# Top-k attention and a low-rank mixer on one core: weighted values of two tiles formed in one go, transposes of u moved two shares

## The chip, the cores and the metric

The kernel runs on one core of a Trainium2 chip. The metric is the device time of one execution in microseconds (us); a kernel's time is the median over its runs. Engines are named as in the profile: PE is TensorE (matmuls; PEld are its weight loads, which overlap them), DVE is VectorE, ACT is ScalarE, POOL is GpSimd, SP is SyncE, which here only issues DMAs. Each engine works through its own queue in the order in which the program gave it work, and waits on semaphores for the others.

## The reference

Attention in which each query keeps only its 32 largest scores, then a mixer over the sequence of rank 32 and a two-layer network over the channels. Eight batches, eight heads, 576 positions, 64 channels a head.

```python
def _attn_ref(q, k, v):                       # (8, 8, 576, 64) each
    scores = scale * np.matmul(q, k.transpose(0, 1, 3, 2))
    kth = np.partition(scores, -32, axis=-1)[..., -32:-31]
    scores = np.where(scores >= kth, scores, -1000000000.0)
    attn = np.exp(scores - np.max(scores, axis=-1, keepdims=True))
    attn = attn / (np.sum(attn, axis=-1, keepdims=True) + 1e-09)
    return np.matmul(attn, v)

def _moe_ref(x, U, V, w_ch1, w_ch2):          # x: heads side by side, (8, 576, 512)
    h = x.transpose(0, 2, 1) @ U @ V          # U (576, 32), V (32, 576)
    u = x + h.transpose(0, 2, 1)
    ch = np.maximum(u @ w_ch1, 0.0) @ w_ch2   # 512 -> 2048 -> 512
    return u + ch
```

## The kernel before

**Tiles and steps.** Heads are taken in pairs g = 0 to 31, four pairs to a batch. The 576 queries of a pair are cut into tiles t = 0 to 3 of 128 rows, for both heads, and a tile 4, the tail, that holds the last 64 rows of both heads. The list `steps` gives each step n one tile; from pair 4 on, tiles 3 and 4 share a step, so that a pair has four steps (`ALONE` = 20 is the first of these). The loop over n at the end of the kernel is an order written out by hand: it emits, in program order, work of several tiles, each at another stage.

**A tile's way.** In step n the loop forms the scores of tile n+1 (`scores`: PE, L336, and L368 for the tail; ACT copies them out, L381, L401, L404), folds each row in two halves (`fold` and `split`: POOL L432, DVE L434, POOL L435), finds the 32 largest of the rows of tile n on DVE (`front`: maxima L487, L502, L520, and replacements L485, L515), and masks and weighs tile n-1 (ACT L546 and L549, POOL L550, ACT L439). DVE turns the weights of tile n-1 in blocks (`blocks`, L576), SP writes them to DRAM (L582), and in the next step ACT's queue fetches them back as PT (`back`, L591). PT has two buffers. In step n PE also forms the weighted values of tile n-3.

**Weighted values.** `weighted(m)` is called early in step m+3, after the first `fill`, with `values` for each tile of step m. `values` takes an accumulator O from the PSUM pool `ps_t` (two buffers, shared by all transposes and by the low-rank products), adds one product over the last 64 keys of both heads with vd (L688, all 128 rows and columns of the array), then eight with va, each for one head and so for 64 columns of the array (L691), and ACT copies O into XT (L700). For the tail there are ten products of 64 columns (L662, ACT L669). Each fp32 product counts as two matmul records in the profile.

**The mixer of a pair.** After the tail's values `weighted` appends `mixed(g, None, 1)` to the list `mixing`. It is a generator that each `fill` moves on by one `yield`: one share of delay (`lag`), then POOL multiplies XT with the inverse sums of the weights into uT (L719 twice, L720 for the tail), then two shares of delay, then PE transposes uT (L725 four times, L738 for the tail) and ACT copies it to X (L729, L739). It then waits until the next `weighted` is done, whereupon PE forms the product with U (pT, L750), and in the next two shares those with V (up, L762), which ACT copies (L777) and POOL adds to uT (L778). With the last pair of a batch uT is whole, and the layers of this batch, `mlp(b)`, go into the list `fillers`.

**Shares of the layers.** Each step calls `fill` eight times. A call adds a share to `due` and then emits matmuls of the layers (first layer L810, second L828, each with a relu or a copy on ACT, L823 and L839; L840 on POOL adds u) until `due` is used up. Twelve layer matmuls after a column block is done, its transposes back are emitted (L852, ACT L854 and L856, SP L858), also through `ps_t`. A share is 1.0227 products of 512 columns; it is multiplied by 1.4 (`LONG`) in the step of tiles 3 and 4, and by 0.91 (`EARLY`) up to step 38. The layers of the last batch are done differently (`closing`), after the last step.

Of the kernel before, what the change touches and what calls it, by code (L numbers as in the profile page):

```python
# [26 lines left out]
def kernel(  # L27
# [35 lines left out]
    NT, TAIL = 4, 64  # L63
# [7 lines left out]
    ALONE = NPAIR * CH  # L71
# [59 lines left out]
    def cols(t):  # L131
        return slice(t * P, t * P + rows(t))
# [4 lines left out]
    def half(h):  # L137
        return slice(h * D, (h + 1) * D)
# [511 lines left out]
                sc[half(h), MAIN:S], rd[2 * NT : 2 * NT + 1, half(h)].to_broadcast([D, TAIL])  # L650
            )

    def values(g, t):

        PT = PTs.pop((g, t))
        va, vd, vt = (a[g % NV] for a in (vas, vds, vts))
        O = ps_t.tile([P, P], F32, tag="tp", name="O")
        if t == NT:
            if g >= NPAIR:
                for j in range(NT + 1):  # L660
                    for h in range(2):
                        nc.tensor.matmul(  # L662
                            O[half(h), 0:TAIL],
                            lhsT=va[:, h, j, :] if j < NT else vt[:, h, :],
                            rhs=PT[:, j, half(h)],
                            start=(j == 0),
                            stop=(j == NT),
                        )
                nc.scalar.copy(XTs[g][:, MAIN:S], O[:, 0:TAIL])  # L669
                return  # L670
            den = dens[g]
            if g not in inverted:
                inverse(g, 2 * NT if g == NPAIR - 1 else 0, 2 * NT + 1)
            for j in range(NT + 1):
                nc.tensor.matmul(
                    O,
                    lhsT=PT[:, j],
                    rhs=va[:, :, j, :] if j < NT else vt,
                    start=(j == 0),
                    stop=(j == NT),  # L680
                )
            for h in range(2):
                nc.scalar.mul(X[half(h), NT, half(h)], O[half(h), half(h)], den[half(h), 2 * NT :])
            return
        if shared(g, t):
            PT = PT.rearrange("p c n -> p (c n)")
            PT = PT.rearrange("p (a c j) -> p c a j", a=4, j=BLK)
        nc.tensor.matmul(O, lhsT=vd, rhs=PT[:, 2 * NT], start=True, stop=False)  # L688
        for j in range(NT):
            for h in range(2):  # L690
                nc.tensor.matmul(  # L691
                    O[half(h)],
                    lhsT=va[:, h, j, :],
                    rhs=PT[:, NT * h + j],
                    start=False,
                    stop=(j == NT - 1),
                )
        if t == 0:
            XTs[g] = attn.tile([P, S], F32, tag="XT", name="XT", bufs=1)
        nc.scalar.copy(XTs[g][:, cols(t)], O)  # L700


    def mixed(g, wait, lag=0):

        for _ in range(lag):
            yield
        b, gi = divmod(g, NPAIR)
        if gi == 0:
            uTs[b] = mlpp.tile([P, NC, S], F32, tag="uT", name="uT")
        XT, den = XTs.pop(g), dens[g]  # L710
        uT = uTs[b][:, gi]
        if g >= NPAIR:
            sc = scales.pop(g)
            pairs_ = [
                a[:, 0:MAIN].rearrange("p (b n) -> p b n", b=2) for a in (XT, sc)
            ]
            ends = [uT[:, OFF[t] : OFF[t] + 2 * P] for t in (0, 2)]
            for i, end in enumerate(ends):
                nc.gpsimd.tensor_tensor(end, pairs_[0][:, i], pairs_[1][:, i], ALU.mult)  # L719
            nc.gpsimd.tensor_tensor(uT[:, at(NT)], XT[:, MAIN:S], sc[:, MAIN:S], ALU.mult)  # L720
            yield
            yield
        tp = ps_t.tile([P, NT, P], F32, tag="tp", name="tp")
        for t in range(NT):
            nc.tensor.transpose(  # L725
                tp[:, t, :], XT[:, cols(t)] if g < NPAIR else uT[:, at(t)], ident
            )
        X4 = X[:, 0:NT, :]
        nc.scalar.copy(X4, tp)  # L729
        if g < NPAIR:  # L730
            X4 = X4.rearrange("p t (h d) -> p t h d", h=2)
            den4 = den[:, 0 : 2 * NT].rearrange("p (t h) -> p t h ()", h=2)
            nc.gpsimd.tensor_tensor(X4, X4, den4.to_broadcast([P, NT, 2, D]), ALU.mult)
        else:
            if g == NPAIR:
                nc.gpsimd.memset(X[TAIL:P, NT, :], 0.0)
            tp = ps_t.tile([P, P], F32, tag="tp", name="tp")
            nc.tensor.transpose(tp[0:TAIL], uT[:, at(NT)], ident)  # L738
            nc.scalar.copy(X[0:TAIL, NT, :], tp[0:TAIL])  # L739
        if wait is None:  # L740
            waiting.append(g)
            while g in waiting:
                yield
        else:
            for _ in range(wait):
                yield
        pT = ps_t.tile([P, P], F32, tag="tp", name="pT")
        for t in range(NT + 1):
            i = t % NT * R
            nc.tensor.matmul(  # L750
                pT[i : i + R, :],
                lhsT=U[:, t, :],
                rhs=X[:, t, :],
                start=(t < NT),
                stop=(0 < t),
            )
        Tb = mlpp.tile([P, P], F32, tag="Tb", name="Tb", bufs=1)
        nc.scalar.copy(Tb, pT)
        yield
        for chunks, (lo, hi) in zip(PARTS, SPAN):  # L760
            up = ps_t.tile([P, WIDE], F32, tag="tp", name="up")
            nc.tensor.matmul(  # L762
                up[:, 0 : hi - lo], lhsT=Tb, rhs=V[:, lo:hi], start=True, stop=(g >= NPAIR)
            )
            for t in chunks if g < NPAIR else ():
                nc.tensor.matmul(
                    up[:, OFF[t] - lo : OFF[t] - lo + rows(t)],
                    lhsT=X[:, t, :],
                    rhs=ident if t < NT else ident2,
                    is_transpose=True if t < NT else None,  # L770
                    start=False,
                    stop=(t == chunks[-1]),
                )
            if g < NPAIR:
                nc.scalar.copy(uT[:, lo:hi], up[:, 0 : hi - lo])
            else:
                nc.scalar.copy(sc[:, lo:hi], up[:, 0 : hi - lo])  # L777
                nc.gpsimd.tensor_tensor(uT[:, lo:hi], uT[:, lo:hi], sc[:, lo:hi], ALU.add)  # L778
            yield
        if gi == NPAIR - 1:  # L780
            fillers.append(closing(b) if b == B - 1 else mlp(b))
# [340 lines left out]
    steps = [[(g, t)] for g in range(NPAIR) for t in range(CH)]  # L1122
    for g in range(NPAIR, NP):
        steps += [[(g, t)] for t in range(NT - 1)] + [[(g, NT - 1), (g, NT)]]
    STEPS = len(steps)
    BATCH = NPAIR * NT


    SLOTS, LONG, EARLY = 8, 1.4, 0.91
    share = MLP_WORK / (NPAIR * SLOTS * (NT - 1 + LONG))  # L1130
    fillers, mixing, due = [], [], 0.0

    def fill(k=1):


        nonlocal due
        for _ in range(k):
            if passes:
                passes.pop(0)()
            if mixing and next(mixing[0], True):  # L1140
                mixing.pop(0)
            due += share * (LONG if len(tiles(n)) > 1 else 1) * (EARLY if n <= ALONE + BATCH + 2 else 1)
            while due > 0:
                if not fillers:
                    due = 0.0
                    break
                done = next(fillers[0], None)
                if done is None:
                    fillers.pop(0)
                else:  # L1150
                    due -= done

    def tiles(n):

        return steps[n] if 0 <= n < STEPS else []

    def weighted(m):

        for g, t in tiles(m):
            values(g, t)  # L1160
        if tiles(m)[-1][1] == NT:
            mixing.append(mixed(g, None, 1) if m < STEPS - 1 else mixed(g, 5, 0))

# [12 lines left out]
    t = 0  # L1176
# [5 lines left out]
    for n in range(STEPS + 2):  # L1182
        if n < STEPS:
            g, t = steps[n][0]
# [9 lines left out]
        if n >= ALONE - 1 and n <= ALONE:  # L1194

            if n < ALONE:
                next(last)
                values(*steps[n - 3][0])
                list(turning)
                next(here)  # L1200
                next(last)
                scores(*steps[n + 1][0])
                fold(*steps[n + 1][0])
                values(*steps[n - 2][0])
            list(turns(*steps[n - 1][0]))
            values(*steps[n - 1][0])
            if n < ALONE:
                split(*steps[n + 1][0])
                next(here)
# [25 lines left out]
        if n < ALONE:  # L1235
# [3 lines left out]
            scores(*steps[n + 1][0])  # L1239
            fold(*steps[n + 1][0])  # L1240
            if n >= 3:
                values(*steps[n - 3][0])
                if (n - 3) % CH == NT:
                    mixing.append(mixed((n - 3) // CH, 3))
            list(turning)
# [111 lines left out]
```

## Time and profile before

| | us |
|---|---|
| median of three runs | 1681.74 (1681.38 to 1683.37) |
| the profiled execution | 1681.84 |
| its span, first to last instruction | 1679.8 |
| busy: PE, DVE, POOL, ACT | 1571.6, 1547.1, 1000.2, 991.1 |
| layers: L810, L828 | 461.7, 462.1 |
| values: L691 | 144.6 |
| scores: L336 | 179.0 |

A row of the profile's groups gives busy time, the mean of one instruction, and the idle time of its engine just before such instructions with what ended it. Matmuls are pipelined, and their modelled ends overlap the next starts: what a run of them costs is read from start to start. A waits row reads: who waited, for whom, microseconds in total, times, longest. The idle time of one engine costs time only where that engine sets the pace.

### The profile page before, as it was taken

What the parts mean: (1) busy time and instruction counts of PE and PEld (TensorE: products, weight loads), DVE (VectorE), ACT (ScalarE), POOL (GpSimd) and SP (SyncE); (2) the same over time, 40 slices, a digit from 0 to 9 for tenths busy, and PEclk for the clock granted to TensorE, in tenths of its full rate; (3) what the DMA queues carried; (4) which work ended last, traced back from release to release, by engine and by line L of the source; (5) the groups of instructions that cost most, each with busy time, mean ns of one, the idle gap of its engine ahead of it and who ended that gap; (6) DMA issues with size and microseconds to landing.
All of it is one profiled execution on the core that took longest, in us unless ns stands there. A gap on an engine that the chain in (4) does not pass through costs nothing.

```text
span 1679.8 us, 30303 instructions
## 1 busy us (share of the span) xinstructions
PE 1571.6 (94%) x9638; PEld 1183.9 (70%) x9638; DVE 1547.1 (92%) x4393; ACT 991.1 (59%) x2475; POOL 1000.2 (60%) x853
## 2 busy tenths in 40 slices
PE   4667698999899999999999999999999999999999
PEld 2444466687667786778777887778777887778776
DVE  7999998999999999999999999999999999994452
ACT  4888788665665556565655656565655656564320
POOL 4778668755666565666566565656666565653620
PEclk7787799999999999999999999999999999999999
DMA  3323232255555555555455455555555555543001
GB/s 87 94 76 97 62 94 73 63 135 132 134 128 135 127 142 132 139 127 138 121 134 137 124 146 132 137 128 136 126 130 136 126 149 132 131 120 110 10 1 28
DMA packets 295631, 189.42 MB, mean 113 GB/s; under 512 B 178768, under 2 KB 279984, under 8 KB 295472
## 3 DMA queue, kind: packets, MB, share of 16 engines
q1 hardware_dynamic: 259728, 117.62, 30.2%
q10 hardware_dynamic: 35744, 69.88, 13.7%
q8 instruction: 76, 1.25, 0.3%
q14 instruction: 83, 0.68, 0.1%
HBM read 116.49 MB, written 70.91 MB: 112 GB/s over the span
## 4 chain that ended last, share of the span: by engine, by line
PE 58%; DVE 25%; POOL 5%; DMA 4%; ACT 3%; issue 2%; SPq 2%; ACTq 0%; DVEq 0%; POOLq 0%
PE mm L828 17%; PE mm L810 16%; DVE m L520 7%; DVE upper L515 7%; PE sc L336 5%; PE O L691 5%; PE mm L904 3%; DVE first L502 2%; DVE y L576 2%; DVE upper L487 2%; PE sc L904 2%; PE tp L904 2%; DMA ld<-in_k_dram 2%; POOL uT L719 2%; PE up L762 1%
## 5 line engine op out<-in xcount | busy, mean ns | idle before, releaser
L550 POOL TENSOR_TENSOR Ssb<-Ssb,E 128x576 f32<-128x576 f32 x243 | 339.9, 1419 | 248.3 <-ACT E L549 247.8
L810 PE MATMUL mm<-uT,w 128*128 128x320 f32 (+1 forms) x1792 | 461.7, 410 | 2.4 <-ACT hT L823 2.0
L828 PE MATMUL mm<-hT,w 128*128 128x320 f32 (+1 forms) x1792 | 462.1, 407 | 0.0
L810 PEld LDWEIGHTS mm<-uT,w 128*128 128x128 f32 x1792 | 335.4, 191 | 103.0 <-issue 11.6
L828 PEld LDWEIGHTS mm<-hT,w 128*128 128x128 f32 x1792 | 332.3, 190 | 93.0 <-issue 10.2
L520 DVE MAX8 m<-upper 128x8 f32<-128x304 f32 (+1 forms) x780 | 367.3, 512 | 0.7
L515 DVE MATCH_REPLACE8 upper<-m,upper 128x304 f32<-128x304 f32 (+1 forms) x520 | 259.9, 507 | 0.0
L432 POOL TENSOR_TENSOR lower<-Ssb 128x576 uint32<-128x576 uint32 x108 | 152.6, 1413 | 139.1 <-ACT Ssb L381 52.2
L439 ACT ACTIVATE Ssb<-Ssb,nmax 128x576 f32<-128x576 f32 x258 | 201.4, 783 | 17.6 <-POOL Ssb L526 9.9
L435 POOL TENSOR_TENSOR lower<-lower,upper 128x576 uint32<-128x576 uint32 x108 | 153.1, 1418 | 74.2 <-DVE upper L434 72.6
L336 PE MATMUL sc<-qkT 64*128 64x288 f32 (+1 forms) x1056 | 179.0, 461 | 11.0 <-ACT Ssb L390 7.8
L487 DVE MAX8 upper<-lower 128x8 f32<-128x288 f32 x432 | 172.3, 440 | 10.7 <-POOL lower L435 10.7
L549 ACT ACTIVATE E<-Ssb,least 128x576 f32<-128x576 f32 x243 | 176.2, 769 | 4.2
L381 ACT COPY Ssb<-sc 128x576 f32<-128x576 f32 x216 | 127.6, 643 | 71.4 <-PE sc L336 71.4
L576 DVE STREAM_TRANSPOSE y<-Ssb 128x512 f32<-128x512 f32 (+1 forms) x312 | 153.9, 545 | 0.0
L823 ACT ACTIVATE hT<-mm 128x320 f32<-128x320 f32 (+1 forms) x224 | 91.9, 411 | 102.1 <-PE mm L810 100.9
L691 PE MATMUL O<-PT,va 128*64 128x128 f32 x2048 | 144.6, 285 | 0.0
L336 PEld LDWEIGHTS sc<-qkT 64*128 64x128 f32 (+1 forms) x1056 | 95.9, 197 | 51.7 <-issue 17.1
L691 PEld LDWEIGHTS O<-PT,va 128*64 128x64 f32 x2048 | 113.4, 141 | 16.4 <-issue 2.0
L700 ACT COPY XT<-O 128x128 f32<-128x128 f32 x128 | 33.8, 264 | 111.3 <-PE O L691 103.8
L515 DVE MATCH_REPLACE8 upper<-first,upper 128x304 f32<-128x304 f32 x216 | 97.7, 460 | 0.0
L485 DVE MATCH_REPLACE8 lower<-upper,lower 128x288 f32<-128x288 f32 x216 | 94.1, 444 | 0.0
(264 smaller groups left out, 2258.3 us busy)
## 6 DMA issues: line engine op xcount, KB each, us to landing
away<-y SPq DMA_DIRECT2D x416, 144.0 KB
PT<-away ACTq DMA_DIRECT2D x104, 576.0 KB
raw<-in_moe_w_ch_dram SPq DMA_DIRECT2D x32, 512.0 KB
va<-in_v_dram SPq DMA_DIRECT2D x64, 128.0 KB
out_dram<-ob SPq DMA_DIRECT2D x59, 128.0 KB
scale<-rd ACTq DMA_DIRECT2D x56, 128.0 KB
ld<-in_q_dram SPq DMA_DIRECT2D x108, 64.0 KB
ld<-in_k_dram SPq DMA_DIRECT2D x108, 64.0 KB
```

The lines of the kernel that those rows point to most:

```text
L336: nc.tensor.matmul(out, lhsT=qkT[half(h), 0, cols(t)], rhs=qkT[half(h), 1, lo:hi], start=True, stop=True,)
L435: nc.gpsimd.tensor_tensor(bottom, bottom, top.bitcast(U32), ALU.subtract)
L439: nc.scalar.activation(E, chunk, AF.Exp, bias=nmax, scale=SCALE, accum_out=total)
L487: nc.vector.max(spot, lower)
L515: nc.vector.match_replace(nxt, ms[c], curs[c], NEG)
L520: nc.vector.max(ms[c], curs[c])
L549: nc.scalar.activation(gap, chunk, AF.Relu, bias=least[:, c : c + 1], scale=-WIDEN)
L550: nc.gpsimd.tensor_tensor(chunk, chunk, gap, ALU.subtract)
L576: nc.vector.transpose(y[:, :, i * NT : i * NT + c].rearrange("p r c j -> p c r j"), E2[:, a : a + c * P].rearrange("p (c r j) -> p c r j", ...
L691: nc.tensor.matmul(O[half(h)], lhsT=va[:, h, j, :], rhs=PT[:, NT * h + j], start=False, stop=(j == NT - 1),)
L810: nc.tensor.matmul(ph[:, 0:w], lhsT=first_layer(cc, f), rhs=uT[:, cc, lo:hi], start=(cc == 0), stop=(cc == NC - 1),)
L828: nc.tensor.matmul(po[:, 0:w], lhsT=w2[:, f, c * P : (c + 1) * P], rhs=hTs[f][:, 0:w], start=(f == 0), stop=(f == NF - 1),)
```

## The change

Three things change in the steps from pair 4 on.

*Values of two tiles.* `values` takes several tiles; its body is now a generator, `valued`, that stops once after the product with vd. For all tiles but a tail the products with vd come first, one after the other, each into its own O; then each tile's products with va follow, and its copy. `weighted` now only keeps the tile in `held` when it is tile 0 or 2 of its pair, and at the next step forms the values of both (tiles 0 and 1, or 2, 3 and 4). The last two steps are formed as before.

*Transposes of u.* In `mixed` the delay between POOL's products and PE's transposes is four shares in place of two, for all but the last pair.

*Shares.* `weight(n)` replaces the factor of a share: from step 24 to the last, 0.18 is taken off it in steps of tile 0 and 2 of a pair, and put on in those of tile 1 and 3. Values that were formed in a step of tile 1 or 3 are those now formed a step later, in one of tile 2 or 0.

```diff
-    def values(g, t):
+    def valued(g, t):
...
+        yield
         for j in range(NT):
             for h in range(2):
                 nc.tensor.matmul(
...
         nc.scalar.copy(XTs[g][:, cols(t)], O)
-
+        yield
+
+
+    def values(*tiles_):
+
+        jobs = [valued(*tile_) for tile_ in tiles_]
+        for job, (_, t) in zip(jobs, tiles_):
+            if t < NT:
+                next(job)
+        for job in jobs:
+            next(job)
...
-            yield
-            yield
+            for _ in range(4 if wait is None else 2):
+                yield
...
+    HEAVY = 0.18
+
+    def weight(n):
+
+        long = LONG if len(tiles(n)) > 1 else 1
+        if n < ALONE + NT or n >= STEPS:
+            return long
+        return long + (-HEAVY if steps[n][0][1] in (0, 2) else HEAVY)
...
-            due += share * (LONG if len(tiles(n)) > 1 else 1) * (EARLY if n <= ALONE + BATCH + 2 else 1)
+            due += share * weight(n) * (EARLY if n <= ALONE + BATCH + 2 else 1)
...
+    held = []
+
     def weighted(m):
 
-        for g, t in tiles(m):
-            values(g, t)
+        g, t = tiles(m)[0]
+        held.extend(tiles(m))
+        if t in (0, 2) and m < STEPS - 2:
+            return
+        values(*held)
+        held.clear()
         if tiles(m)[-1][1] == NT:
             mixing.append(mixed(g, None, 1) if m < STEPS - 1 else mixed(g, 5, 0))
```

The other calls of `values` (pairs 0 to 3, one tile at a time) are only rewritten for its new form.

## The prediction

> **What bounds the kernel now.** I read the page first: busy shares, then the forty slices.
>
> ```profile
> span 1679.8 us, 30303 instructions
> ...
> PE 1571.6 (94%) x9638; PEld 1183.9 (70%) x9638; DVE 1547.1 (92%) x4393; ACT 991.1 (59%) x2475; POOL 1000.2 (60%) x853
> ...
> PE   4667698999899999999999999999999999999999
> ...
> DVE  7999998999999999999999999999999999994452
> ```
>
> Two engines are full together from the eighth slice (about 300 us) to the 36th (1512 us). Only in the last slices does DVE run empty while PE goes on. Shares over a whole run hide which of the two waits, so next come the busy times of two stretches of 189.2 us, the period in which the trace repeats itself: one batch, that is four pairs of heads (columns: stretch, length, then busy time of PE, PEld, DVE, ACT, POOL, granted clock, DMA share, GB/s).
>
> ```profile
> 756.20:945.40 189.20, 187.59 (x1189) 143.13 (x1188) 186.14 (x565) 112.24 (x284) 113.85 (x97) 1.00 0.53 133
> 945.40:1134.60 189.20, 187.60 (x1189) 143.13 (x1188) 186.10 (x565) 112.24 (x284) 113.88 (x97) 1.00 0.53 133
> ```
>
> Of 189.2 us DVE idles 3.1, PE by this view 1.6. The change takes no work from DVE: a batch can't become shorter than 186.1 us. Third, who waits, from 300 to 1536 us: the DVE's waits, and the PE's.
>
> ```profile
> DVE upper L434 <- ACT Stail L401: 12.1, 10, 1.9
> DVE upper L487 <- POOL lower L435: 6.2, 7, 1.9
> ```
>
> ```profile
> PE tp L725 <- POOL uT L719: 11.9, 35, 3.1
> PE mm L810 <- ACT hT L823: 2.0, 3, 1.3
> PE O L688 <- DMA PT<-away: 1.0, 1, 1.0
> ```
>
> DVE waits 18.3 us in all, two thirds of it at L434 for scores that PE had just formed. So PE sets the pace, DVE close behind. PE's own waits are nearly all at one line, the transposes of u, L725. Idle time understates them, as a matmul's modelled end runs on; the starts say more. The timeline of PE around one such place (start, length, engine, line):
>
> ```profile
> 704.17 1.24 PE L336 MATMUL sc<-qkT 64*128 64x288 f32 x8
> 705.34 2.96 PE L828 MATMUL mm<-hT,w 128*128 128x320 f32 x10
> 708.46 0.44 PE L725 MATMUL tp<-ident,uT 128*128 128x128 f32 x2 [0.16 <-POOL uT L719]
> 709.16 0.44 PE L725 MATMUL tp<-ident,uT 128*128 128x128 f32 x2 [0.26 <-POOL uT L719]
> 709.44 0.30 PE L738 MATMUL tp<-ident,uT 128*64 128x128 f32 x1
> 709.58 3.40 PE L828 MATMUL mm<-hT,w 128*128 128x320 f32 x12
> 712.81 0.49 PE L852 MATMUL tp<-ident,oT 128*128 128x128 f32 x3
> 713.14 1.78 PE L828 MATMUL mm<-hT,w 128*128 128x320 f32 x6
> 714.75 0.38 PE L688 MATMUL O<-PT,vd 128*128 128x128 f32 x2
> 715.07 1.09 PE L691 MATMUL O<-PT,va 128*64 128x128 f32 x16
> ```
>
> Twelve L828 last 3.23 us from start to start (709.58 to 712.81), so one is 0.27 and the ten before L725 need 2.70: L725 could start at 708.04 and starts at 708.46, 0.42 late. Three transposes of L852 take 0.33 (712.81 to 713.14), so four need 0.44; here L725 to L738 is 0.98, another 0.54. **Loss: 0.96 us a pair.** What is late is POOL, in the all-engine timeline of the same place:
>
> ```profile
> 704.97 1.18 ACT L381 COPY Ssb<-sc 128x576 f32<-128x576 f32 x2 [1.65 <-PE sc L336]
> ...
> 706.28 1.42 POOL L432 TENSOR_TENSOR lower<-Ssb 128x576 uint32<-128x576 uint32 x1 [1.35 <-DMA away<-y]
> ...
> 707.65 1.46 POOL L719 TENSOR_TENSOR uT<-XT,scale 128x256 f32<-128x256 f32 x2
> ...
> 709.03 0.35 POOL L720 TENSOR_TENSOR uT<-XT,scale 128x64 f32<-128x64 f32 x1
> ```
>
> PE's scores (until 705.41) release ACT's copy L381 (until 706.15), that releases POOL's L432, and behind it in POOL's queue stand L719 twice and L720 (until 709.38). The transposes need all three. The loop starts and ends on PE, so it isn't DVE's doing.
>
> **The change, part by part.** *Transposes two shares later.* Today three shares (fill 2 to 4) lie between the scores and L725; after it five, but each is 0.82 of itself, since this is a step of tile 2. A whole share is 1.0227 columns-of-512, 2 x 0.432 us each (a 320-wide matmul pair lasts 0.54, so 512 columns 0.86): 0.88 us. Three whole shares are 2.65, five of 0.82 are 3.62: L725 comes 0.96 us later after the scores, and L720, the last thing it needs, is 0.96 late today. It just covers. Matmuls come whole (0.54 or 0.43), so some pairs keep a few tenths; bounds of the saving 0.5 and 0.96, I take 0.85 (the arithmetic lies near the upper end). What is moved with them: ACT's copies L729 and L739 (0.59 and 0.26), and the three shares after. The next reader, pT (L750), is at 716.09 today, 5.7 us after L739 ends. After the change two light shares, one of 1.58 and no values stand between: 2 x 0.72 + 1.39 = 2.8 us, against 1.1 for the two copies. No DMA and no POOL work moves.
>
> *Values of two tiles together.* No matmul is added or removed. From start to start: L688 (two, full array) 0.32 to L691, where two full-array matmuls of 128 columns alone would be 0.22 (L852: 0.109 each): 0.10 goes at the change of array shape. L691 to L336 or L750 is 1.02 (715.07 to 716.09), but to L662, which has the same shape, 0.92 to 0.93 (701.38 to 702.31): again 0.10. Two tiles apart: 2 x (0.32 + 1.02) = 2.68; together 0.22 + 0.32 + 0.92 + 1.02 = 2.48. Against that the light step now goes from full-array layers straight into scores of 64 rows, a passage that the trace doesn't hold. Bounds of the net saving per two tiles: 0 (it costs two such changes) to 0.20 (nothing); I take 0.10, one change more, as both passages seen cost that. That is 0.2 us a pair. The Trainium skill, TensorEngine Tiling (Array Packing), section Key Properties, says that changing the tiling mode, not just the tile, drains the array; by it the light step pays too and 0.10 is right, while the two rows alone would promise 0.20. *Buffers:* O takes both buffers of ps_t at once, and the tail a third; ACT's copy L700 (0.26) must free the first before L662. Today's rows: values start at 701.07, so the first tile's end would be 702.5, the second's 703.45; L700 runs from 702.64 to 702.89. Cover 0.5 us; if ACT is later, PE waits, and behind it the tail scores, then L434. The Trainium skill, TensorEngine Tiling (Array Packing), section PSUM Bottleneck, warns that tiling speeds up TensorE but not the emptying of PSUM, which speaks against holding two accumulators; by it the cover would be gone and a pair 0.26 us worse, where the row (0.26 us in a gap of 0.92) says nothing is lost. PT's row for tile 0 is held a step longer, and ACT's DMA into that buffer (L591) then waits for values that stand ahead of L381's scores in PE's order, so L381, ahead of it on ACT, covers it. XT's one buffer is refilled for tile 0 a step later than today, behind L720 all the same. SP's loads of va and vd go into the buffers of three pairs back, whose values are done either way.
>
> *Shares dealt.* Per pair the weights still sum to 4.4. A step is 7.07 us of layers by weight 1; 0.18 is 1.27 us, about the 1.24 to 1.34 of a tile's values. So scores in steps 0 and 2 keep their place, and those in 1 and 3 come 2 to 3 us earlier (values gone, and the lighter shares before them). PE waits there if DVE's L434 hasn't freed the scores' buffers: L434 ends at 707.43, the next scores are at 716.65, elsewhere at least 5.2 us after. Enough.
>
> **Sum.** PE per pair -0.85 - 0.2 = -1.05, per batch 189.2 - 4.2 = 185.0, below DVE's 186.1. So DVE takes over and the gain is what DVE waits today. L434's 12.1 us I count in full: PE gains 1.05 a pair, and the largest wait, about 1.6, comes once in four pairs. L487's 6.2 I count by half: POOL's L435 stands behind L840, which hangs on ACT's DMA issues as well as on PE. Gain 12.1 + 3.1 = 15.2: span 1664.6. The profiled execution took 1681.84, 2.0 above its span (median of the runs 1681.74): **1666.6, say 1667 us.** What follows the last step is PE's closing with the same work, and moves up whole. Its own range: from all 18.3 us won and 2 more at the end, where DVE stands 6.5 us at L629 (1661) to half of L434's (1675).
>
> **Rivals.** *Transposes still wait* (the change doesn't do what it says): smaller shares eat the delay, 0.2 to 0.35 us a pair remain as gain. For it: the cover is exact to 0.0. Against: every wait shortens by what L725 is moved. 27 pairs x 0.2 to 0.35 = 5 to 9, so about 1675. *DVE holds its waits* (gain hidden anyway): DVE is at 98.4%, and waits at L487 hang on POOL. For it: from 331 to 565 us DVE waits nowhere. Against: L434's waits follow PE's scores directly. 2 to 3 us off, 1680. *The third accumulator* (slower): at the step of tile 2 the tail's O waits for L700, which on ACT stands behind L546 and two L549 (1.65 us), and these for DVE's last maxima. For it: the less PE waits elsewhere, the further it runs ahead of DVE, and so of ACT. Against: cover 0.5 us, and a lead of PE that is lost there costs DVE nothing at first. It decides from 0.5 + 1.05 us of lateness on; at 2 us, 27 x (2 - 0.5 - 1.05) = 12: 1694.
>
> **Chances.** Forecast 0.66, transposes still wait 0.14, DVE holds its waits 0.08, third accumulator 0.12. A measurement of this kernel tells 0.2% (3.4 us) from no change: faster 0.80, same 0.08, slower 0.12. The range 1661 to 1680 leaves out the slower case, half of the unchanged one and a little at the bottom.
>
> **What would show it.** Right: no wait at L725, DVE over 99.5% busy in a batch of some 186.5 us, L434's waits gone, PE waiting here and there for ACT or for scores' buffers. L688 four in a row at every other step, L691 to L691 0.92. Wrong: new waits of L662 or L688 on L700, L750 on L739, or a batch still near 189 us with DVE's waits moved to the scores after three tiles' values.

## The result, and the profile after

The changed kernel takes 1697.19 us in the median (1691.11 to 1702.04), the kernel before 1681.5 in the same measurement: a ratio of 1.0093, 95% interval 1.0082 to 1.0104. It is slower where 1667 us was forecast, and its runs spread over 11 us where those of before spread over 3. The profiled execution took 1691.11, its span 1689.0. It is the fastest of the six, so the profile can show 9.2 of the 15.7 us that the medians lie apart.

The page of the changed kernel, busy shares and slices:

```profile
span 1689.0 us, 30294 instructions
...
PE 1558.2 (92%) x9638; PEld 1179.3 (70%) x9638; DVE 1548.1 (92%) x4393; ACT 986.0 (58%) x2475; POOL 1001.6 (59%) x853
...
DVE  7999997999999999999999999999999999994452
```

PE's busy time is 13.4 us shorter than before, and yet the end comes 9.2 us later. A batch of four pairs (columns: stretch, length, busy time of PE, PEld, DVE, ACT, POOL, granted clock, DMA share, GB/s):

```profile
763.00:952.40 189.40, 185.56 (x1190) 142.45 (x1188) 186.01 (x564) 111.11 (x285) 114.11 (x96) 1.00 0.54 133
```

It takes 189.4 us, of which DVE works the same 186.0. From one L434 to the one four pairs on, batches take 187.4 to 191.0 us, before 187.5 to 189.5. So in the middle of the run nothing was won. Where the 9 us were lost shows in the start of L434 for tile 3 of single pairs, in both traces:

| before, us | after, us | later by |
|---|---|---|
| 331.3 | 336.4 | 5.1 |
| 377.8 | 385.7 | 7.9 |
| 754.8 | 764.5 | 9.7 |
| 1133.1 | 1141.9 | 8.7 |
| 1511.5 | 1520.2 | 8.7 |

Nearly all of it is lost by 380 us; from there on L434 of tile 3 is 7.4 to 10.6 us later than before. The DVE's waits, and the PE's, from 300 to 1545 us:

```profile
DVE upper L434 <- ACT Stail L401: 22.5, 15, 4.0
DVE upright L629 <- ACT den L560: 1.6, 1, 1.6
DVE upper L487 <- POOL lower L435: 0.4, 1, 0.4
```

```profile
PE mm L823 <- ACT hT L836: 22.9, 16, 2.3
PE tp L738 <- POOL uT L732: 2.6, 1, 2.6
```

The line numbers have moved: L823 is the first layer (L810 before), L836 its relu (L823 before), L738 the transposes of u (L725 before). Those wait no more, but 22.9 us of waits for a relu stand in their place, and DVE's waits for the tail's scores have grown from 12.1 to 22.5 us. One belongs to the other. The chain of waits around one such place, in order of time (start, length, what):

```profile
749.72 0.59 SPq L258
750.32 0.04 issue
750.36 5.07 DMA ld<-in_k_dram
755.42 0.02 issue
755.45 0.49 ACTq L649
755.93 0.05 issue
755.98 0.20 ACT nmax L506
756.19 0.28 ACT hT L836
756.47 0.04 issue
756.51 1.56 PE mm L823 x6
758.07 0.45 PE O L690 x4
758.52 1.90 PE O L694 x32
760.42 0.58 PE O L662 x20
761.00 1.18 PE sc L368 x14
762.18 0.71 PE sc L336 x4
762.89 0.02 issue
762.91 1.18 ACT Ssb L381 x2
764.09 0.39 ACT Stail L401
764.48 0.02 issue
764.50 0.76 DVE upper L434
```

It starts at a load of k. ACT's queue in the same stretch:

```profile
752.80 0.62 ACTq L645 DMA_DIRECT2D scale<-rd  x1
755.45 0.49 ACTq L649 DMA_DIRECT2D scale<-rd  x1
755.98 0.20 ACT L506 ACTIVATE nmax<-first 128x2 f32<-128x2 f32 x1 [3.50 <-DMA ld<-in_k_dram]
756.09 0.64 ACT L836 ACTIVATE hT<-mm 128x256 f32<-128x256 f32 x2
```

In the step of tile 1, now a light one (it forms no values; its shares of the layers are the larger ones, of 1.18), ACT issues four DMAs that fetch the inverse sums (`scale`, L645 and L649 twice). Three follow each other at 0.66 us. The fourth stands for 2.0 us, until 755.45. It needs nothing of k: the program tells the end of its DMAs by eight semaphores in turn, and this DMA gets the one that the load of k issued at 750.36 used last. That load's last update is at 755.42, 0.02 us before ACT goes on. Behind it in ACT's queue stand two relus. PE has two buffers for its layers, both full, and stands 1.75 us. The time that PE was to win in the light step is lost, and the heavy step comes: values of three tiles, then the tail's scores, then L434, which has waited 1.80 us when it starts at 764.50.

In the changed kernel the fourth DMA stands in 23 of 26 pairs, 43.5 us in all; before it stood in 9 of 27, 13.9 us. Each of these stands ends 0.02 us after the DMA that used its semaphore last has landed: in the changed kernel 17 times a load of k, and 6 times ACT's own fetch of PT (L591); before, 3 and 6 times. Twelve of PE's 16 waits for a relu, some 20 of the 22.9 us, end 1.0 to 1.3 us after such a DMA goes out. Before, the semaphore had mostly been used last by a load of k that had landed already. The four DMAs of one such pair before:

```profile
790.65 0.62 ACTq L645 DMA_DIRECT2D scale<-rd  x1
791.31 0.63 ACTq L649 DMA_DIRECT2D scale<-rd  x1
791.97 0.62 ACTq L645 DMA_DIRECT2D scale<-rd  x1
792.63 0.62 ACTq L649 DMA_DIRECT2D scale<-rd  x1
```

The load in question was issued at 788.36, 2.3 us ahead of the first of the four, and had landed at 790.80. In the changed kernel the lead is 1.1 us (750.36 to 751.49): ACT's DMAs follow the load sooner, and the fourth meets it still under way.

### The profile page after: what moved, and what is told of

Read it like the earlier page. It is cut to its first block, busy times and chain, and to the rows that moved or that the text cites. A ratio compares the mean times of both kernels' runs of the same rounds, so it can differ in the third digit from the quotient of the medians.

```text
span 1689.0 us, 30294 instructions
## 1 busy us (share of the span) xinstructions
PE 1558.2 (92%) x9638; PEld 1179.3 (70%) x9638; DVE 1548.1 (92%) x4393; ACT 986.0 (58%) x2475; POOL 1001.6 (59%) x853
## 4 chain that ended last, share of the span: by engine, by line
DVE 60%; PE 18%; DMA 10%; SPq 5%; ACT 2%; issue 2%; POOL 1%; ACTq 1%; DVEq 0%; POOLq 0%
DVE m L520 15%; DVE upper L515 14%; DVE y L576 7%; DMA ld<-in_k_dram 6%; DVE upper L487 6%; DVE first L502 5%; DVE lower L485 4%; DVE place L515 3%; PE mm L917 3%; PE mm L841 3%; DVE upper L434 3%; PE mm L823 3%; DVE qkT L306 2%; PE O L694 2%; PE tp L917 2%
## 5 line engine op out<-in xcount | busy, mean ns | idle before, releaser
L823 PE MATMUL mm<-uT,w 128*128 128x320 f32 (+1 forms) x1792 | 464.2, 410 | 23.0 <-ACT hT L836 22.9
L823 PEld LDWEIGHTS mm<-uT,w 128*128 128x128 f32 x1792 | 334.4, 191 | 127.0 <-ACT hT L836 32.2
L520 DVE MAX8 m<-upper 128x8 f32<-128x304 f32 (+1 forms) x780 | 376.9, 537 | 0.7
L515 DVE MATCH_REPLACE8 upper<-m,upper 128x304 f32<-128x304 f32 (+1 forms) x520 | 266.1, 532 | 0.0
L435 POOL TENSOR_TENSOR lower<-lower,upper 128x576 uint32<-128x576 uint32 x108 | 153.0, 1417 | 187.8 <-DVE upper L434 187.7
L439 ACT ACTIVATE Ssb<-Ssb,nmax 128x576 f32<-128x576 f32 x258 | 201.5, 783 | 32.1 <-POOL lower L432 13.9
L487 DVE MAX8 upper<-lower 128x8 f32<-128x288 f32 x432 | 176.1, 459 | 4.3 <-POOL lower L435 4.3
L549 ACT ACTIVATE E<-Ssb,least 128x576 f32<-128x576 f32 x243 | 176.4, 769 | 4.3
L836 ACT ACTIVATE hT<-mm 128x320 f32<-128x320 f32 (+1 forms) x224 | 90.3, 409 | 89.1 <-PE mm L823 81.4
L694 PE MATMUL O<-PT,va 128*64 128x128 f32 x2048 | 132.4, 282 | 0.0
L434 DVE TENSOR_TENSOR upper<-sc,Ssb 128x576 f32<-128x576 f32 x108 | 83.0, 769 | 24.4 <-ACT Stail L401 24.4
```

The lines of the kernel that those rows point to most:

```text
L439: nc.scalar.activation(E, chunk, AF.Exp, bias=nmax, scale=SCALE, accum_out=total)
L487: nc.vector.max(spot, lower)
L515: nc.vector.match_replace(nxt, ms[c], curs[c], NEG)
L520: nc.vector.max(ms[c], curs[c])
L549: nc.scalar.activation(gap, chunk, AF.Relu, bias=least[:, c : c + 1], scale=-WIDEN)
L694: nc.tensor.matmul(O[half(h)], lhsT=va[:, h, j, :], rhs=PT[:, NT * h + j], start=False, stop=(j == NT - 1),)
```

## The experiments

Theory A: the loss comes from ACT, held by that DMA in the light step, so that PE can't lay up time for the heavy one. Theory B: values of three tiles ahead of the tail's scores make L434 late whatever ACT does. Medians and ratios are each against the kernel before on the same chip.

**Transposes alone**, an edit of the kernel before.

```diff
-            yield
-            yield
+            for _ in range(4 if wait is None else 2):
+                yield
```

> The kernel before with four shares of delay in place of two ahead of the transposes of u (L725), nothing else changed. Theory A (the loss comes from ACT: in the light step of tile 1 it now stands at the fourth of its DMAs for the inverse sums until a load of k has landed, relus behind it, so PE cannot use the light step) and theory B (the loss comes from the order: values of three tiles ahead of the tail's scores make L434 late whatever ACT does) agree here: PE's waits at L725 go, 0.85 to 0.96 us a pair, DVE takes over, 1667 to 1673 us. If the moved transposes are themselves the cause of the loss, 1690 us or more.

Measured: 1686.38 us, ratio 1.0025 (1.0012 to 1.0037). Neither faster nor the cause of the whole loss. Its waits, DVE's and PE's, from 300 to 1545 us:

```profile
DVE upper L434 <- ACT Stail L401: 12.2, 7, 4.5
DVE upper L487 <- POOL lower L435: 7.5, 6, 2.6
```

```profile
PE mm L810 <- ACT hT L823: 14.1, 11, 3.3
PE O L688 <- DMA PT<-away: 6.4, 7, 1.6
```

The waits at L725 are gone here too (3.3 us left, 3.1 of it at one place), and DVE waits as long as before. Instead ACT's fourth DMA now stands in 19 of 27 pairs, 32.8 us, and PE waits for relus. The expectation of both theories was wrong: this wait holds PE without any pairs of tiles and without dealt shares.

**Pairs of tiles and dealt shares alone** (the two `yield`s of before put back into the changed kernel).

> The changed kernel with the two shares of delay of before: values of two tiles together and shares of 0.82 and 1.18 alone. A and B: slower than before, and slower than the changed kernel by up to the L725 waits, 1695 to 1715 us, L434 waiting at the step of tile 2. If the pairs cost nothing by themselves, within 5 us of 1681.

Measured: 1707.15, ratio 1.0154 (1.0137 to 1.0171). As expected: with PE waiting for the transposes again (25.0 us), L434 waits 38.2.

**Even shares**, from here on edits of the changed kernel where nothing else is said.

```diff
-    HEAVY = 0.18
+    HEAVY = 0.0
```

> The changed kernel with HEAVY 0: all shares as before, so heavy steps are 1.3 us longer on PE and light ones 1.3 us shorter. B: the scores after the values of three tiles come 1.3 us later still, once or twice a pair for 27 pairs, 1715 to 1740 us. A: PE reaches the light step's DMAs later by nothing and finds them blocked as often, PE's waits at L823 as in the changed kernel, 1695 to 1715. If the dealt shares are the cause of the loss, 1665 to 1680.

Measured: 1705.79, ratio 1.0147 (1.0117 to 1.0177). The dealt shares are worth some 8 us to the changed kernel, less than B asked for and within A's range; they aren't its fault.

**The four DMAs at the end of the step.**

```diff
-        if n < STEPS and n - 2 >= ALONE and len(tiles(n - 2)) > 1:
-            scale(steps[n - 2][0][0])
         next(here, None)
         next_params(1)
...
         next(here, None)
         fill()
+        if n < STEPS and n - 2 >= ALONE and len(tiles(n - 2)) > 1:
+            scale(steps[n - 2][0][0])
         fill()
```

> The changed kernel with the four DMAs for the inverse sums (L645, L649) issued by ACT at the end of the step, ahead of its last share, in place of ahead of L506. A: the waits of two to three us at the fourth of them go, with them PE's waits at L823 (22.9 us) and most of L434's (22.5 us): 1668 to 1682 us. B: PE's waits at L823 may go, L434 still waits: 1688 to 1702.

Measured: 1685.12, ratio 1.0023 (1.0014 to 1.0032): 12 us of the 16 return. That lies between the ranges of A and B. PE's waits for relus fall from 22.9 to 2.8 us, for A, but L434 still waits 14.9 us for the tail's scores (22.5 in the changed kernel). Another wait of PE takes the relus' place:

```profile
PE O L662 <- ACT XT L703: 14.5, 15, 2.1
PE O L690 <- DMA PT<-away: 3.2, 3, 1.3
```

L662 is the tail's values, L703 ACT's copy of the accumulator of tile 2 (L700 before): the third accumulator waits for a buffer of `ps_t`, as the issues of four DMAs now stand just ahead of L546 and L549 on ACT.

**Only the fourth DMA at the end of the step.** The first three stay; `ends_` is the L649 of before.

```diff
+    fourths = []
...
-            nc.scalar.dma_start(
+            ends_ = lambda h=h: nc.scalar.dma_start(
                 sc[half(h), MAIN:S], rd[2 * NT : 2 * NT + 1, half(h)].to_broadcast([D, TAIL])
             )
+            if h == 0 or g == NP - 1:
+                ends_()
+            else:
+                fourths.append(ends_)
...
         fill()
+        while fourths:
+            fourths.pop()()
         fill()
```

> The changed kernel with only the fourth of the four DMAs (the second L649) moved to the end of the step; the first three stay. If the wait of this one DMA for the load of k is what costs (theory A), it gives what moving all four gave, 1683 to 1688 us. If the issue time of four DMAs on ACT (0.66 us each) at that place is what costs, only a quarter of it, 1692 to 1699.

Measured: 1673.62, ratio 0.9960 (0.9946 to 0.9975). **One DMA of 16 KB, moved by three shares, is worth some 22 us** by the ratios; the changed kernel is then faster than before. That is 9 us under the range of theory A, which had taken over the time of the run above, and far from the 1692 us and more that four issue times would leave. The DMA still stands (22 of 27 pairs, 35.3 us), but L506 and the relus of three shares stand ahead of it in ACT's queue, no longer behind. With three issues fewer ahead of L546 and L549 PE waits 4.4 us for the third accumulator in place of 14.5, and L434 5.6 us for the tail's scores. The waits of PE in this kernel (L829 is the first layer, L668 the tail's values):

```profile
PE mm L829 <- ACT hT L842: 4.7, 7, 1.8
PE O L668 <- ACT XT L709: 4.4, 7, 1.0
```

**The DMAs' place in the kernel before**: the move of the four, in the kernel before.

> The kernel before with the four DMAs for the inverse sums issued at the end of the step, nothing else changed. There the fourth stands two to three us in one pair of four, without a PE wait behind it. Theory A: worth 0 to 4 us, 1678 to 1682. If the DMAs' place is worth as much to the kernel before as to the changed one (12 us), 1670.

Measured: 1678.08, ratio 0.9979 (0.9968 to 0.9990), as expected. The place by itself is worth 3 us there; PE still stands at L725 (14.3 us, 43 times).

**Transposes and late DMAs**, no pairs.

> The kernel before with four shares of delay ahead of the transposes of u and the four DMAs at the end of the step. Theory A: in the run with the transposes alone PE's waits only moved from L725 (43.9 us with its weight loads) to the relus behind these DMAs (L810, 14.1 us); with both gone DVE takes over and its waits fall under 8 us: 1668 to 1675. If the forecast of DVE taking over was wrong for another reason, 1680 to 1687.

Measured: 1664.69, ratio 0.9890 (0.9866 to 0.9915), 13.4 us below the run just above and 3 us under theory A's range. Two batches of it, and DVE's waits at L434 and L487 from 300 to 1545 us:

```profile
749.10:935.30 186.20, 185.37 (x1187) 143.32 (x1187) 185.94 (x566) 111.65 (x284) 113.28 (x97) 1.00 0.52 135
935.30:1121.10 185.80, 185.80 (x1191) 143.92 (x1190) 185.66 (x565) 112.38 (x287) 114.06 (x97) 1.00 0.53 136
```

```profile
DVE upper L434 <- ACT Stail L401: 2.7, 2, 2.1
DVE upper L487 <- POOL lower L435: 0.4, 1, 0.4
```

A batch takes 186.0 us and DVE is busy for 185.8 of them: now it sets the pace, as forecast.

**Transposes and only the fourth DMA late.**

> The kernel before with four shares of delay ahead of the transposes of u and only the fourth DMA at the end of the step. Theory A: as with all four moved, 1663 to 1668 us. If ACT's issue time counts: 1670 to 1680.

Measured: 1663.84, ratio 0.9900 (0.9884 to 0.9917). As with all four, so it is the one DMA's wait and what is queued behind it. This kernel and the one above are among the fastest; their intervals overlap.

**Pairs of tiles from pair 6 on** (pairs 4 and 5 turn their weights on PE, through `ps_t`).

```diff
-        if t in (0, 2) and m < STEPS - 2:
+        if t in (0, 2) and ALONE + 2 * NT <= m < STEPS - 2:
...
-        if n < ALONE + NT or n >= STEPS:
+        if n < ALONE + 3 * NT or n >= STEPS:
```

> The changed kernel, but tiles are formed together and shares dealt only from pair 6 on (pairs 4 and 5 as before; these turn their weights on PE through the two buffers of ps_t). The trace of the changed kernel has lost 5.1 us against before by 331 us and 7.9 by 378 us. If that comes from two accumulators against the turns of pairs 4 and 5, some 4 to 6 us return: median 1690 to 1693 us. If it comes from the order of values and scores in any pair, nothing returns: 1695 to 1699.

Measured: 1687.61 (1681.43 to 1694.35), ratio 1.0032 (1.0011 to 1.0052). That is 10 us below the changed kernel's first measurement and 2 us under the lower of the two ranges; the spread of both kernels is as large, so the size is uncertain.

**Late DMAs and pairs from pair 6 on.**

> The changed kernel with the DMAs at the end of the step and pairs of tiles from pair 6 on, the tail's accumulator as in the change (a third buffer). Moving the DMAs alone gave 1685.1 us, all three mends 1665.2. The late DMAs alone had lost 8.0 us by 331 us: if that is pairs 4 and 5, 1675 to 1679, and the rest (10 us) is the third accumulator.

Measured: 1674.61, ratio 0.9969 (0.9956 to 0.9982); 9 to 10 us below the late DMAs alone (by the ratios, by the medians). PE still waits 10.8 us for the third accumulator.

**Late DMAs and two buffers for three accumulators.** The tail's accumulator is the second half of tile 3's, and ACT copies tile 3 after the tail's products.

```diff
+    rests = {}
...
-        O = ps_t.tile([P, P], F32, tag="tp", name="O")
+        if t == NT and g >= NPAIR:
+            O = rests.pop(g)
+        else:
+            both = ps_t.tile([P, 2, P], F32, tag="tp", name="O")
+            O = both[:, 0]
+            if t == NT - 1 and g >= NPAIR:
+                rests[g] = both[:, 1]
...
+        if t == NT - 1 and g in rests:
+            yield
...
+        for job in jobs:
+            next(job, None)
```

> The changed kernel with the DMAs at the end of the step and the tail's accumulator in the second half of tile 3's, pairs of tiles from pair 4 on as in the change. If the third accumulator is worth 10 us beside the late DMAs: 1673 to 1678, with PE's 14.5 us at L662 gone. If pairs 4 and 5 are all that is left: 1684.

Measured: 1668.99, ratio 0.9933 (0.9918 to 0.9948). 15 to 16 us from the accumulator beside the late DMAs, where 10 were expected, and the wait for it is gone. L434 waits 2.4 us for the tail's scores, with pairs of tiles from pair 4 on.

**All three mends.**

> The changed kernel with three mends: the DMAs at the end of the step, pairs from pair 6 on, and the tail's accumulator in the second half of tile 3's, so that two buffers hold all three (ACT copies tile 3 after the tail's products). In the run with the late DMAs alone PE waited 14.5 us for a third buffer and lost 8 us by 331 us. If these are what is left of the loss: 1668 to 1676. If L434's waits come from the three tiles' values themselves: 1680 to 1686.

Measured: 1665.24, ratio 0.9898 (0.9869 to 0.9928), 3 us under the first range. DVE's waits for the tail's scores, from 300 to 1540 us:

```profile
DVE upper L434 <- ACT Stail L401: 2.7, 2, 2.2
```

They are down to 2.7 us with the values of three tiles still ahead of those scores. Theory B falls: that order is harmless where PE can lay up time. And the mended pairs bring nothing beyond the transposes (1664.69): by then DVE sets the pace.

## Why the prediction was wrong

**Right, by the runs.** The loss at L725 and its mending: the waits went from 11.9 to 2.6 us. No run shows a batch under 185.8 us, and with the four DMAs late the transposes gave 13.4 us (1678.08 to 1664.69), near the 15.2 of the sum. Also the terms on array shape. PE of the changed kernel at a light step:

```profile
744.09 1.89 PE L823 MATMUL mm<-uT,w 128*128 128x256 f32 x8
745.92 1.24 PE L336 MATMUL sc<-qkT 64*128 64x288 f32 x8
```

Eight matmuls of 0.216 are 1.73 us, the scores start after 1.83: the passage straight into scores of 64 rows costs 0.10, as taken.

**The step that failed** is the end of *Shares dealt*: that in light steps PE could only be held by the scores' buffers, "Enough". The forecast looked for what holds PE itself, and not for what holds ACT, on which PE's layers hang by two buffers. The change brought ACT sooner after the load to a DMA issue whose wait is set by another transfer, and there ACT stood, and PE behind it. The dealt shares aren't needed for it: with the transposes alone the fourth DMA stands 32.8 us in place of 13.9, so "No DMA and no POOL work moves" in *Transposes two shares later* failed in the same way. No DMA changed its place in a queue, but their times against each other did. In the sum it is the sentence "So DVE takes over and the gain is what DVE waits today": of the 1.05 us a pair that PE was to save (28 us in 27 pairs) 22.9 stand again as waits for relus. The sum named ACT's DMA issues, at L487, as a thing that POOL's L840 hangs on, ahead of L435, counted half of 6.2 us for it, and didn't ask what their wait was; in the before trace it could be seen in 9 pairs of 27.

**The rivals.** That of the third accumulator was real, but small in the changed kernel: 0.4 us at L662 from 300 us on, and one wait ahead of that, at the first tail formed this way:

```profile
280.93 0.69 PE L662 MATMUL O<-PTt,va 128*64 128x64 f32 x16 [1.94 <-ACT XT L703]
```

It came out when the four DMAs were moved (14.5 us, and 15 to 16 us of time when this was mended too). Most of that came from their new place ahead of L546 and L549: with only the fourth moved it is 4.4 us. So the rival had the right place and the right order on ACT, but needed these issues for its size. "Transposes still wait" was wrong: L725's waits went, and no time came of it. "DVE holds its waits" came nearest, though it named POOL, and it was ACT that held PE, and PE DVE: L487's waits went from 6.2 to 0.4, L434's from 12.1 to 22.5.

**The first pairs** weren't forecast at all. L434 is 2.9 us late by 285 us, just after the wait at 280.93 above, 5.1 by 331 and 7.9 by 378. Between the last two PE stands for relus twice, 1.80 and 1.95 us, the second time behind the fourth DMA, and then has a granted clock of 0.61 from 374.7 to 378.1; the kernel before has 1.00 from 300 to 425. The kept traces tell part of the loss by 378 us: with late DMAs it is 8.7, with the accumulator's mend beside them 5.1, with pairs from pair 6 on beside them 1.0, with all three mends nothing. So pairs of tiles in pairs 4 and 5 go with some 5 us that the accumulator's mend doesn't give back; that it is two accumulators against the turns of these pairs was not shown, and the cause stays open. The clock may be a part of it: the run with pairs from pair 6 on alone has lost 6.8 us by 378, and its clock was 0.51 from 292.2 to 299.0 and 0.52 from 370.9 to 377.7.

## What to carry to other kernels

When a wait is taken from the engine that sets the pace, look for the next thing that stops it one engine away: the relus or copies that empty its buffers, and everything queued ahead of them. A DMA issue on a compute engine's queue is such a place, since it can wait for a transfer that has nothing to do with it; put it where little is queued behind. And before time is moved between steps, check that the engine can run ahead in the light ones.

## What the hardware showed

Half the clock can follow a short stand of PE. At the longest wait of L434 in the changed kernel (4.03 us, at 1332.89) PE had stood 2.23 us for a relu. The two stretches around it (columns as above, granted clock behind POOL's busy time):

```profile
1320.90:1324.30 3.40, 1.17 (x6) 0.92 (x6) 3.40 (x11) 1.52 (x5) 0.17 (x1) 1.00 0.55 106
1324.40:1327.70 3.30, 3.30 (x23) 2.89 (x23) 3.30 (x14) 0.67 (x2) 2.77 (x2) 0.50 0.83 192
```

In 3.4 us PE was busy 1.17, and for the next 3.4 it ran at half speed: the values of tiles 2 and 3 took 3.7 us (1324.98 to 1328.63) in place of 2.3 (757.91 to 760.25). The Trainium skill, TensorE: Matmul & The Clock Gate, section Why this matters for your kernels, warns of idle gaps beyond some 3 us; here it came after 2.2, while a wait of 2.31 us at 945.99 left the clock at 1.00 (945 to 950). So the length of the wait alone doesn't decide. That such windows fall differently from run to run would explain the spread of 11 us; the runs' mean clocks (0.965 at 1691 us, 0.958 at 1702) point that way, but only one run was profiled.

In that one profile DVE's instructions are recorded some 20 to 30 ns longer (L520 537 ns in the mean against 512), though a pair at DVE's own pace takes 46.4 to 46.5 us as before; no other kernel shows it. The mean of a row is no measure of pace; start to start is.
